# Six uses for a chunk's v product, spread over the steps, and an earlier start of the second phase

## The chip, the core and the metric

The kernel runs on one core of a Trainium2 chip. The core has five engines with a queue of instructions each: TensorE (PE; matmuls, with PEld for its weight loads), VectorE (DVE), ScalarE (ACT), GpSimd (POOL) and SyncE (SP), which here only issues DMAs. An engine takes its instructions in order and waits for others by semaphores. The metric is the device time of one execution in microseconds, the median of several.

## The reference

Inputs: q, k, v of 4 batches x 12 heads x 448 rows x 64; w_pre and w_post 12 x 12; w_in 768 x 2048, w_out 2048 x 768 and alpha 2048.

```
scores = q k^T / 8                                    per batch and head, 448 x 448
scores = einsum('bhij,hg->bgij', scores, w_pre)       heads mixed
attn   = softmax(scores over j)
attn   = einsum('bhij,hg->bgij', attn, w_post)        heads mixed again
x      = attn v, heads side by side                   1792 x 768
h      = x w_in
out    = (max(h, 0) + alpha min(h, 0)) w_out          1792 x 768
```

The weights w_in and w_out arrive as 64-bit floats and are rounded to 32 bits on the chip (the conversion).

## The kernel before

**First phase: attention.** A batch's 448 query rows are cut into four chunks (three of 120 rows, one of 97 of which the last 90 are used), 16 chunks in all, `ci`. A chunk is cut into groups of 10 rows x 12 heads, 180 in all, and a step `m` handles the two groups 2m and 2m+1. What a chunk and a step need is done by these functions:

- `qk(ci, p)`: score products of two heads of the chunk, a *use* of the bank pair `ps_s` (one buffer, two PSUM banks); `qk_out` lets ACT copy them to the SBUF tile `st`. Six per chunk.
- `relay`: a DMA that lays a group's scores out with (row, head) on the partitions, to `sr`, some steps ahead.
- `mix(m)`: the product with w_pre (TensorE) into one of two buffers of `ps_m`; `rmax` (DVE) and `exp` (ACT, two calls) follow; `norm` (DVE) folds the sum and w_post into a small factor `r`.
- `post(m)`, two steps later: the product of e and r, into `pa` (one buffer); `post_out` lets ACT copy it to the chunk's `at`.
- `pv(ci, half)`: the chunk's product with v, in two halves of three head pairs; both halves are uses of one `ps_s` tile, and `pv_out` copies both banks after the second half, each in one ACT copy of 3 x 120 columns. The result goes to the DRAM tensor `x2` by a DMA on SP.
- `convert`: the rounding of the weights on DVE, seven operations for each of 32 tiles, some two or three per step, fetched and stored (`wsc`) by SP.

`step(m)` records all this in a fixed order (the schedule is written by hand, `manual_schedule`); a step has two places for uses, one between mix and post and one after post. The table `places` says which use stands where: both halves of a chunk's `pv` in the step when its last group is through `post`, the six `qk` of the chunk ahead two to a step in the steps left. So there are three kinds of steps: with both halves of a `pv`, with two `qk`, and with nothing (L285 to L298).

**Second phase: the two layers.** It starts after the last step, in buffers that are opened once all pools of the first phase are closed. For each batch (`xs`, x transposed, 768 x 448) and each of 16 slices of 128 of the 2048 (a unit, 64 in all): `l1` multiplies with the slice of w_in, `act` applies the activation, `l2` multiplies with the slice of w_out and accumulates in six banks. Each value is split in a high and a low part, so each layer takes 18 matmuls per unit. `load_x` and `split_x` bring x from `x2` (DVE splits), `load_w` and `split_w` the weights from `wsc` (ACT writes the high part, POOL the low one). The loads of the first x stand on SP behind everything of the first phase.

Of the kernel before, what the change touches and what calls it, by code (L numbers as in the profile page):

```python
# [37 lines left out]
WARM = (12, 8)  # L38
X_FROM = 9
# [22 lines left out]
def talking_heads_prelu(ctx: ExitStack, tc: tile.TileContext, q, k, v, w_pre, w_post, mask, w_in, w_out, alpha, out):  # L62
# [18 lines left out]
    x2 = dpool.tile([NCC, 128, NT], F32, name="x2")  # L81
    wsc = dpool.tile([NFC, 128, 2 * DM], F32, name="wsc")
# [3 lines left out]
    p1 = ExitStack()  # L86
    pool = lambda name, bufs, **kw: p1.enter_context(tc.tile_pool(name=name, bufs=bufs, **kw))
    cvp = pool("cvp", 2)
    kp = pool("kp", 2)
    qp = pool("qp", 3)  # L90
    sp = pool("sp", 2)
# [8 lines left out]
    ps_m = pool("ps_m", 2, space=PSUM)  # L100
    ps_s = pool("ps_s", 1, space=PSUM)
    ps_a = pool("ps_a", 1, space=PSUM)
# [114 lines left out]
    def pv(ci, half):  # L217


        b, c = chunk_list[ci]  # L220
        cn = ROWS[c][1] * GI
        if half == 0:
            u_t["pv", ci] = ps_s.tile([128, 2, 512], F32, tag="s", name=f"x{ci}")
        ps = u_t["pv", ci]
        for cl in range(3):
            for s in range(NS):
                for t in range(2):
                    h = 2 * (3 * half + cl) + t
                    nc.tensor.matmul(ps[64 * t:64 * t + 64, half, cl * CW:cl * CW + cn], v_t[b][:, s, h * D:(h + 1) * D],  # L229
                                     a_t[ci][:, s, h, :cn], start=(s == 0), stop=(s == NS - 1))  # L230

    def pv_out(ci, half):

        if half == 0:
            return
        b, c = chunk_list[ci]
        r0, st = ROWS[c]
        c0, cn = CHUNKS[c][0] + r0, st * GI
        xe = xep.tile([128, NCC, CW], F32, tag="xe", name=f"xe{ci}")
        ps = u_t.pop(("pv", ci))  # L240
        for bank in range(2):
            src = ps[:, bank, :3 * CW].rearrange("p (c i) -> p c i", c=3)[:, :, :cn]
            nc.scalar.copy(xe[:, 3 * bank:3 * bank + 3, :cn].rearrange("p c (i g) -> p c i g", i=GI),
                           src.rearrange("p c (g i) -> p c i g", i=GI))
        later.append(lambda: nc.sync.dma_start(
            out=x2[:, :, b * S + c0:b * S + c0 + cn].rearrange("c p i -> p c i"), in_=xe[:, :, :cn]))
# [3 lines left out]
    def convert():  # L250
# [9 lines left out]
        def store_c(f, x, t):  # L260
            nc.sync.dma_start(out=wsc[f, :, x * DM:(x + 1) * DM], in_=t.bitcast(F32))
# [23 lines left out]
    places = {}  # L285
    for ci in range(NC):
        m = (first[ci + 1] - 1) // 2 + LAG + 1
        places[m, 0], places[m, 1] = ("pv", ci, 0), ("pv", ci, 1)
    for ci in range(1, NC):
        m1 = laid_out(first[ci]) - 1  # L290
        m0 = laid_out(first[ci - 1]) + 1 if ci > 1 else -1
        room = [(m, i) for m in range(m0, m1 + 1) for i in range(2) if (m, i) not in places]

        room.sort(key=lambda x: ((x[0], 1 - x[1]) in places or (x[0], 1 - x[1]) in room and x[1] == 1, x))
        room += [(m0 - 1, i) for i in range(2) if (m0 - 1, i) not in places]
        assert len(room) >= NP
        for p, x in enumerate(sorted(room[:NP])):
            places[x] = ("qk", ci, p)  # L298
# [10 lines left out]
    with tc.manual_schedule():  # L309
# [62 lines left out]
        def use(place, out):  # L372
            if place in places:
                f, *args = places[place]
                {"qk": (qk, qk_out), "pv": (pv, pv_out)}[f][out](*args)


        def step(m):
# [10 lines left out]
            use((m - 1, 1), 1)  # L389
            use((m, 0), 0)  # L390
# [13 lines left out]
            if live(m - LAG):  # L404
                post_out(m - LAG)
# [152 lines left out]
```

## Time and profile before

| | us |
|---|---|
| median of 3 runs | 931.94 (928.97 to 932.42) |
| profiled execution | 936.22, span 934.4 |
| first phase's steps, 35.7 to 418.8 | 383.1, TensorE busy 325.1 |
| from there to the second phase's steady run, 461.5 | 42.7 |
| second phase, 461.5 to 930.4 | 468.9, TensorE busy 468.9 |

A row of the timeline gives the start, the duration, the engine, the line, the operation with its output and inputs, how many instructions are merged in it, and in brackets the idle time before it with what ended it. "issue" as the releaser means that the engine waited for nothing that the profile shows. Matmuls of 32-bit floats in the first phase are recorded as two each, so a use of `qk` shows as 8 matmuls, one half of `pv` as 48, and `post` as 56. The spans of matmuls overlap; what one costs is better read from start to start.

### The profile page before, as it was taken

Reading aid. Unit: us, or ns where it says so; the run is one execution under the profiler, and the core shown is the slowest. Engines: PE = TensorE matmul, PEld = TensorE weight load, DVE = VectorE, ACT = ScalarE, POOL = GpSimd, SP = SyncE. Lnnn points to the kernel's source line nnn. Section 1 sums busy time; section 2 is a strip of 40 time slices with the busy share of each in tenths; the row PEclk is TensorE's granted clock in tenths of the full one; section 3 lists DMA queues with packets and bytes.
Section 4 is the critical chain, followed back from the end, with each engine's and each line's share of the span. In section 5 each row is a group of like instructions: output and inputs, shape, how many; then the busy total and the mean of one; then the engine's idle time right before and its main releaser. Section 6 shows DMA issues by size and latency. Waiting matters only on the chain.

```text
span 934.4 us, 23967 instructions
## 1 busy us (share of the span) xinstructions
PE 840.6 (90%) x10388; PEld 665.0 (71%) x10388; DVE 486.1 (52%) x856; ACT 438.1 (47%) x870; POOL 355.8 (38%) x315
## 2 busy tenths in 40 slices
PE   5779897798779989875699999999999999999998
PEld 3255563565555556545599999999999999999997
DVE  4758767587667878770522355223552236522222
ACT  1758877487757868753222233222233322322231
POOL 2323322132222323300554455555544455454442
PEclk9999999899999999999799999999999999999999
DMA  6999789988996897632770002000020000100001
GB/s 171 236 257 279 234 252 251 242 241 254 253 263 225 249 278 224 217 107 82 307 296 1 11 11 98 2 0 2 19 73 26 1 1 21 43 17 1 1 1 60
DMA packets 55158, 123.90 MB, mean 133 GB/s; under 512 B 26028, under 2 KB 32988, under 8 KB 55052
## 3 DMA queue, kind: packets, MB, share of 16 engines
q1 hardware_dynamic: 39846, 81.71, 29.2%
q0 software_dynamic: 14208, 37.56, 14.4%
q10 hardware_dynamic: 998, 3.09, 1.1%
q8 instruction: 82, 1.34, 0.6%
q14 instruction: 24, 0.20, 0.1%
HBM read 59.96 MB, written 23.62 MB: 89 GB/s over the span
## 4 chain that ended last, share of the span: by engine, by line
PE 69%; ACT 12%; issue 9%; DMA 5%; DVE 3%; POOL 1%; SPq 0%; ACTq 0%; POOLq 0%; DVEq 0%
PE acc L487 25%; PE h L462 25%; PE x L229 9%; ACT e L183 6%; PE s L146 4%; ACT st L154 4%; PE pa L205 3%; DMA sr<-st 3%; PE m L171 2%; ACT at L215 2%; DMA xr<-x 1%; POOL sr L163 1%; DMA wb<-in_w_post_dram 1%; DVE nm L176 1%; DVE ce L57 0%
## 5 line engine op out<-in xcount | busy, mean ns | idle before, releaser
L462 PE MATMUL h<-xs,wi 128*128 128x448 f32 x1152 | 251.1, 371 | 13.7 <-DVE xs L452 12.1
L487 PE MATMUL acc<-g,wo 128*128 128x448 f32 x1152 | 248.3, 368 | 0.0
L462 PEld LDWEIGHTS h<-xs,wi 128*128 128x128 f32 x1152 | 217.8, 189 | 36.7 <-issue 12.3
L487 PEld LDWEIGHTS acc<-g,wo 128*128 128x128 f32 x1152 | 216.3, 188 | 21.8
L163 POOL DMA_DIRECT2D sr<-st x174 | 108.2, 622 | 293.1 <-PE m L171 238.0
L440 POOL TENSOR_TENSOR wi<-wr,wi 128x768 fp32r<-128x768 f32 x64 | 118.6, 1853 | 263.4 <-ACT wi L439 263.4
L471 DVE TENSOR_SCALAR t<-h,alpha_sb 128x448 f32<-128x448 f32 x64 | 43.8, 684 | 245.4 <-PE h L462 245.4
L473 ACT CAST g<-t 128x448 fp32r<-128x448 f32 x64 | 36.3, 567 | 275.0 <-DVE t L472 275.0
L176 DVE TENSOR_REDUCE nm<-m 128x2 f32<-128x896 f32 x90 | 97.8, 1087 | 92.2 <-PE m L171 91.9
L205 PEld LDWEIGHTS pa<-r,e 64*64 64x64 f32 x5040 | 102.5, 138 | 55.4 <-issue 33.8
L440 POOL TENSOR_TENSOR wo<-wr,wo 128x768 fp32r<-128x768 f32 x64 | 123.9, 1935 | 7.6 <-ACT wo L439 5.9
L215 ACT COPY at<-pa 128x480 f32<-128x480 f32 x180 | 93.4, 576 | 59.1 <-PE pa L205 58.8
L205 PE MATMUL pa<-r,e 64*64 64x60 f32 x5040 | 106.8, 225 | 14.4 <-issue 9.0
L146 PE MATMUL s<-k,q 64*64 64x448 f32 (+2 forms) x768 | 100.7, 577 | 19.3 <-ACT st L154 11.9
L183 ACT ACTIVATE e<-m,nm 128x448 f32<-128x448 f32 x180 | 113.6, 644 | 5.1 <-DVE nm L176 3.0
L171 PE MATMUL m<-sr,wk 64*64 64x448 f32 x720 | 92.6, 566 | 18.5 <-ACT e L183 10.4
L229 PE MATMUL x<-at,v 128*64 128x120 f32 (+1 forms) x1536 | 86.7, 268 | 22.5 <-issue 19.8
L229 PEld LDWEIGHTS x<-at,v 128*64 128x64 f32 x1536 | 77.8, 140 | 36.6 <-issue 21.9
L154 ACT COPY st<-s 120x896 f32<-120x896 f32 (+1 forms) x93 | 84.8, 912 | 31.7 <-PE s L146 29.0
L439 ACT CAST wo<-wr 128x768 fp32r<-128x768 f32 x64 | 53.8, 841 | 62.3 <-PE acc L487 62.3
L146 PEld LDWEIGHTS s<-k,q 64*64 64x64 f32 (+2 forms) x768 | 22.6, 130 | 64.0 <-ACT st L154 42.6
L474 DVE TENSOR_TENSOR g<-t,g 128x448 fp32r<-128x448 f32 x64 | 40.7, 636 | 44.0 <-ACT g L473 44.0
(40 smaller groups left out, 484.8 us busy)
## 6 DMA issues: line engine op xcount, KB each, us to landing
sr<-st POOLq DMA_DIRECT2D x174, 210.0 KB, 7.0
cr<-in_w_in_dram SPq DMA_DIRECT2D x16, 768.0 KB, 6.6
cr<-in_w_out_dram SPq DMA_DIRECT2D x16, 768.0 KB, 7.8
wsc<-ct SPq DMA_DIRECT2D x32, 384.0 KB, 7.4
wr<-wsc SPq DMA_DIRECT2D x14, 768.0 KB, 10.2
xr<-x SPq DMA_DIRECT2D x24, 224.0 KB, 4.7
out_dram<-o SPq DMA_DIRECT2D x24, 224.0 KB, 2.0
k<-in_k_dram SPq DMA_DIRECT2D x21, 224.0 KB, 12.9
```

The source lines that it names most:

```text
L146: nc.tensor.matmul(ps[lo:hi, hf, :S], q_t[ci][r, p, lo:hi], k_t[b][r, p, :], start=True, stop=True)
L154: copy(dst[:cn, p], u_t.pop(("qk", ci, p))[:cn, :, :S])
L163: dma.dma_start(out=sr_t[n][SR0:SR0 + GP], in_=s_t[ci][r0:r0 + (GI - 1) * st + 1:st])
L171: nc.tensor.matmul(ps[hf:hf + 64, u, :S], wk[r, :], g[r, :], start=True, stop=True)
L176: nc.vector.tensor_reduce(out=nm, in_=m_t[m][:, :, :S], axis=AX.X, op=ALU.max, negate=True)
L183: nc.scalar.activation(out=e_t[m][:, u], in_=m_t[m][:, u, :S], func=AF.Exp, bias=nm_t[m][:, u:u + 1], scale=1.0, accum_out=se_t[m][:, u:u ...
L205: nc.tensor.matmul(dst[:, :, HI * u:HI * u + HI], e[h, u, 64 * jb:64 * jb + 64], r[h, u].rearrange("p (h i) -> p h i", h=H), start=True, s ...
L215: nc.scalar.copy(dst, pa[:, g, :NS * GP].rearrange("p (s i) -> p s i", i=GI))
L229: nc.tensor.matmul(ps[64 * t:64 * t + 64, half, cl * CW:cl * CW + cn], v_t[b][:, s, h * D:(h + 1) * D], a_t[ci][:, s, h, :cn], start=(s == ...
L440: nc.gpsimd.tensor_tensor(t[:, 1], w, t[:, 0], ALU.subtract)
L462: nc.tensor.matmul(ps[:, :S], w[:, tw, cc * 128:(cc + 1) * 128], x[:, tx, cc, :], start=(i == 0), stop=(i == 3 * NCC - 1))
L487: nc.tensor.matmul(accs[c][:, :S], w[:, tw, c * 128:(c + 1) * 128], g[:, tg], start=(f == 0 and i == 0), stop=(f == NFC - 1 and i == 2))
```

## The change

Two parts. First, `pv` of a chunk becomes six uses, one for each head pair, each with its own copy of one bank's 120 (or 90) columns into `xe`; the DMA to `x2` follows the sixth. A use may stand in any step of a window: for `pv` from the step after the chunk's last `post` to the step in which a tile of `at` is written again, for `qk` as before. An assignment (`cost`, six rounds over all uses) moves each use to the step of its window with the fewest others, preferring steps without its own kind. A step may now have any number of uses: the first between mix and post, the second after post, more behind the copy of the one before.

Second, the tensors `x2` and `wsc` become a tensor per batch and per slice. The pools that the scores and inputs used (`cvp`, `kp`, `qp`, `sp`) lie on the right side of SBUF and are closed at step M0 = 87; in their place open `xs0`, `xr`, `wi`, `wo`, `wr0`, `gp` of the second phase. The loads of the first batch's x and of three slices' weights stand there on SP, their splits in steps 88 and 89. After the last step, `post` 88, `l1` of unit 0, `post` 89, `l1` of unit 1 and the last chunk's six `pv` follow each other, then `l2` of unit 0 in another order of its banks.

```
-        for cl in range(3):
-            for s in range(NS):
-                for t in range(2):
-                    h = 2 * (3 * half + cl) + t
-                    nc.tensor.matmul(ps[64 * t:64 * t + 64, half, cl * CW:cl * CW + cn], ...)
+        ps = ps_s.tile([128, 2, 512], F32, tag="s", name=f"x{ci}_{i}")
+        for s in range(NS):
+            for t in range(2):
+                h = 2 * i + t
+                nc.tensor.matmul(ps[64 * t:64 * t + 64, 0, :cn], v_t[b][:, s, h * D:(h + 1) * D],
+                                 a_t[ci][:, s, h, :cn], start=(s == 0), stop=(s == NS - 1))
...
+        nc.scalar.copy(xe[:, i, :cn].rearrange("p (i g) -> p i g", i=GI),
+                       u_t.pop(("pv", ci, i))[:, 0, :cn].rearrange("p (g i) -> p i g", i=GI))
...
+        spread("qk", ci, laid_out(first[ci - 1]) + 1 if ci > 1 else -1, laid_out(first[ci]) - 1)
+        spread("pv", ci - 1, (first[ci] - 1) // 2 + LAG + 1, first[ci + 1] // 2 + LAG if ci + 1 < NC else NB - 1)
+    def cost(t, m):
+        there = [x[0] for x in tasks if x is not t and x[4] == m]
+        late = m == t[3] and t[0] == "pv" and len(there) > 1
+        return (late, 2 * len(there) + there.count(t[0]), m)
...
+            for u, v in zip(us[1:], us[2:]):
+                use(u, 1)
+                use(v, 0)
+            pending.extend(us[1:][-1:])
...
+        for m in range(-1, NB):
+            if m == M0:
+                ...
+                p1r.close()
+                open_early()
+                xq += [load_x(0, cc) for cc in range(3)]
+                load_w(0)
+                xq.append(load_x(0, 3))
+                load_w(1)
+                load_w(2)
+            step(m)
+            if m > M0:
+                for cc in range(3 * (m - M0 - 1), 3 * (m - M0)):
+                    split_x(0, cc, xq.pop(0))
+                    if cc + 4 < NCC:
+                        xq.append(load_x(0, cc + 4))
+                split_w(m - M0 - 1, 0)
+        p1m.close()
+        P2["h"] = pl("h", 2, space=PSUM, side="right")
+        while pending:
+            use(pending.pop(), 1)
+        norm(NB - 1)
+        post(NB - 2)
+        post_out(NB - 2)
+        split_w(0, 1)
+        ps = l1(0)
+        post(NB - 1)
+        post_out(NB - 1)
+        act(0, ps)
+        ps = l1(1)
+        for i in range(NP):
+            pv(NC - 1, i)
+            pv_out(NC - 1, i)
+        act(1, ps)
+        for f in later:
+            f()
+        ...
+        load_w(3)
+        load_w(4)
+        split_w(1, 1)
+        split_w(2, 0)
+        l2(0)
```

TensorE's queue before, in the middle of the first phase: two steps without a use, then a step with both halves of a chunk's v product and the mix of the next (m is mix, pa is post, x the v product, s the score product; x24 are 24 matmuls of the program).

```order
L171 MATMUL m_5307<-sr_116,wk 64x448 x2
L171 MATMUL m_5307<-sr_117,wk 64x448 x2
L205 MATMUL pa<-r_5259,e_5195 64x12x5 x28
L171 MATMUL m_5359<-sr_110,wk 64x448 x2
L171 MATMUL m_5359<-sr_111,wk 64x448 x2
L205 MATMUL pa<-r_5316,e_5263 64x12x5 x28
L171 MATMUL m_5414<-sr_112,wk 64x448 x2
L171 MATMUL m_5414<-sr_113,wk 64x448 x2
L229 MATMUL x_5420<-at_4997,v_119 64x120 x24
L205 MATMUL pa<-r_5367,e_5320 64x12x5 x28
L229 MATMUL x_5420<-at_4997,v_119 64x120 x24
```

The same engine after, in the same part: two steps, each with one score product ahead of post and a sixth of a v product behind it.

```order
L173 MATMUL m_5257<-sr_130,wk 64x448 x2
L173 MATMUL m_5257<-sr_131,wk 64x448 x2
L148 MATMUL s_3_5264<-k_3692,q_4833 64x448 x2
L148 MATMUL s_3_5264<-k_3692,q_4833 56x448 x2
L207 MATMUL pa<-r_5201,e_5136 64x12x5 x28
L230 MATMUL x_1_5311<-at_4828,v_136 64x90 x8
L173 MATMUL m_5329<-sr_132,wk 64x448 x2
L173 MATMUL m_5329<-sr_133,wk 64x448 x2
L148 MATMUL s_4_5336<-k_3692,q_4833 64x448 x2
L148 MATMUL s_4_5336<-k_3692,q_4833 56x448 x2
L207 MATMUL pa<-r_5272,e_5205 64x12x5 x28
L230 MATMUL x_2_5383<-at_4828,v_136 64x90 x8
```

The v product has left its own step and stands where a step had a second score product or nothing.

SP's queue before, at the seam of the phases: the stores of the last three chunks' x and of the last converted weights, then the second phase's loads of x (xr) and weights (wr).

```order
L245 DMA x_57<-xe_5925 128x6x120
L261 DMA wsc<-ct_0_5815 128x768
L245 DMA x_57<-xe_6267 128x6x120
L245 DMA x_57<-xe_6424 128x6x90
L261 DMA wsc<-ct_1_5973 128x768
L447 DMA xr_0_6473<-x_57 128x448
L447 DMA xr_1_6475<-x_57 128x448
L447 DMA xr_2_6477<-x_57 128x448
L447 DMA xr_3_6479<-x_57 128x448
```

The same queue after.

```order
L245 DMA x_3_60<-xe_5676 128x6x120
L261 DMA wsc_76<-ct_0_5948 128x768
L261 DMA wsc_76<-ct_1_6077 128x768
L461 DMA xr_0_6282<-x_0_57 128x448
L461 DMA xr_1_6284<-x_0_57 128x448
L461 DMA xr_2_6286<-x_0_57 128x448
L446 DMA wr_6288<-wsc_61 128x1536
L461 DMA xr_3_6290<-x_0_57 128x448
L446 DMA wr_6292<-wsc_62 128x1536
L446 DMA wr_6294<-wsc_63 128x1536
L245 DMA x_3_60<-xe_5981 128x6x120
```

Four loads of x and three of weights have moved ahead of the stores of the last three chunks.

TensorE's queue after, at the seam (h is the first layer's product, 18 matmuls a unit): the last uses of the chunk before the last, then posts and first-layer products in turn, and the last chunk's uses.

```order
L230 MATMUL x_4_6454<-at_5943,v_137 64x120 x8
L207 MATMUL pa<-r_6371,e_6317 64x12x5 x28
L230 MATMUL x_5_6501<-at_5943,v_137 64x120 x8
L207 MATMUL pa<-r_6466,e_6375 64x12x5 x28
L476 MATMUL h_6564<-xs_6281,wi_6450 128x448 x18
L207 MATMUL pa<-r_6529,e_6468 64x12x5 x28
L476 MATMUL h_6619<-xs_6281,wi_6518 128x448 x18
L230 MATMUL x_0_6638<-at_6351,v_137 64x90 x8
L230 MATMUL x_1_6649<-at_6351,v_137 64x90 x8
```

Before, all h stood behind the last chunk's x; now two units' h stand between the posts and ahead of that x.

## Rows read from the trace of the kernel before

**Rows 1.** Windows by stage: stretch, length, each engine's busy us, clock, DMA share, GB/s.
```profile
35.70:418.80 383.10, 325.09 (x7524) 208.15 (x7516) 282.32 (x562) 275.67 (x628) 104.42 (x168) 0.97 0.86 240
418.80:437.70 18.90, 14.58 (x424) 12.92 (x424) 2.93 (x11) 8.18 (x21) 0.00 (x0) 1.00 0.08 23
...
461.50:930.40 468.90, 468.90 (x2269) 425.63 (x2268) 173.06 (x236) 138.35 (x199) 236.01 (x125) 1.00 0.10 37
```

**Rows 2.** Timeline of TensorE, three kinds of steps: start, duration, line, operation, wait.
```profile
299.71 2.68 PE L229 MATMUL x<-at,v 128*64 128x120 f32 x48
302.32 0.98 PE L171 MATMUL m<-sr,wk 64*64 64x448 f32 x8
...
306.19 0.93 PE L171 MATMUL m<-sr,wk 64*64 64x448 f32 x8
307.39 0.98 PE L146 MATMUL s<-k,q 64*64 64x448 f32 x8 [0.28 <-ACT st L154]
308.20 1.09 PE L205 MATMUL pa<-r,e 64*64 64x60 f32 x56
...
310.23 0.93 PE L171 MATMUL m<-sr,wk 64*64 64x448 f32 x8
...
314.28 0.93 PE L171 MATMUL m<-sr,wk 64*64 64x448 f32 x8
...
316.73 0.98 PE L171 MATMUL m<-sr,wk 64*64 64x448 f32 x8 [0.60 <-ACT e L183]
```

**Rows 3.** Waits of TensorE: total us, times, longest.
```profile
PE x L229 <- issue: 19.8, 9, 4.5
...
PE s L146 <- ACT st L154: 11.9, 33, 1.1
...
PE pa L205 <- issue: 9.0, 7, 2.2
PE m L171 <- DMA sr<-st: 7.1, 4, 5.1
```

**Rows 4.** Timeline of TensorE, two neighbouring issue waits.
```profile
270.25 0.63 PE L229 MATMUL x<-at,v 128*64 128x120 f32 x7 [1.69 <-issue]
...
278.56 1.86 PE L205 MATMUL pa<-r,e 64*64 64x60 f32 x55 [2.11 <-issue]
```

**Rows 5.** DMA queues of the page: packets, MB, share of 16 engines.
```profile
q8 instruction: 82, 1.34, 0.6%
```

**Rows 6.** Groups of the page: busy us, mean ns, idle before.
```profile
L440 POOL TENSOR_TENSOR wi<-wr,wi 128x768 fp32r<-128x768 f32 x64 | 118.6, 1853 | 263.4 <-ACT wi L439 263.4
...
L154 ACT COPY st<-s 120x896 f32<-120x896 f32 (+1 forms) x93 | 84.8, 912 | 31.7 <-PE s L146 29.0
L439 ACT CAST wo<-wr 128x768 fp32r<-128x768 f32 x64 | 53.8, 841 | 62.3 <-PE acc L487 62.3
```

**Rows 7.** Tile xe: ns min/median/max, first and last start, forms.
```profile
L243 ACT COPY xe<-x x32: 384/459/466, 69.7 to 438.0; 128x360 f32<-128x360 f32 x24, 128x270 f32<-128x270 f32 x8
```

**Rows 8.** Timeline of TensorE at the seam.
```profile
418.81 0.98 PE L171 MATMUL m<-sr,wk 64*64 64x448 f32 x8 [1.20 <-ACT e L183]
...
433.71 3.94 PE L229 MATMUL x<-at,v 128*64 128x90 f32 x96 [1.13 <-ACT at L215]
449.78 0.71 PE L462 MATMUL h<-xs,wi 128*128 128x448 f32 x1 [12.12 <-DVE xs L452]
```

**Rows 9.** The chain that ended last, its last long piece.
```profile
922.96 7.45 PE acc L487 x36
```

**Rows 10.** Timeline of SP's queue at the seam.
```profile
426.98 11.79 SPq L245 DMA_DIRECT2D x<-xe  x2
...
439.40 13.68 SPq L447 DMA_DIRECT2D xr<-x  x6
```

**Rows 11.** Tile xs: ns min/median/max of cast and subtraction.
```profile
L452 DVE CAST xs<-xr x24: 379/386/1787, 447.8 to 806.5; 128x448 fp32r<-128x448 f32 x24
L453 DVE TENSOR_TENSOR xs<-xr,xs x24: 624/2153/2162, 449.7 to 807.0; 128x448 fp32r<-128x448 f32 x24
```

More of the change, by code (lines that the diff above doesn't have):

```diff
@@ L38 @@
 WARM = (12, 8)
+W_EARLY = 3
 X_FROM = 9
@@ L238, in pv_out @@
         c0, cn = CHUNKS[c][0] + r0, st * GI
[L239 to L246, printed above, removed]
+        if i == 0:
+            xe_t[ci] = xep.tile([128, NCC, CW], F32, tag="xe", name=f"xe{ci}")
+        xe = xe_t[ci]
+        nc.scalar.copy(xe[:, i, :cn].rearrange("p (i g) -> p i g", i=GI),
+                       u_t.pop(("pv", ci, i))[:, 0, :cn].rearrange("p (g i) -> p i g", i=GI))
+        if i == NCC - 1:
+            later.append(lambda: nc.sync.dma_start(
+                out=x2[b][:, :, c0:c0 + cn].rearrange("c p i -> p c i"), in_=xe[:, :, :cn]))
     later = []
@@ L281, in laid_out, with spread @@
         return max(n // 2 - RAHEAD - 1, 0 if n < first[1] else 3)
[L285 to L288, printed above, removed]
+    uses, tasks = {}, []
+    def spread(f, ci, m0, m1):
+        tasks.extend([f, ci, m0, m1, m0 + i % (m1 - m0 + 1)] for i in range(NP))
     for ci in range(1, NC):
[L290 to L298, printed above, removed]
+        spread("qk", ci, laid_out(first[ci - 1]) + 1 if ci > 1 else -1, laid_out(first[ci]) - 1)
[4 more added lines that the diff above has]
+        return (late, 2 * len(there) + there.count(t[0]), m)
+    for _ in range(NP):
+        for t in tasks:
+            t[4] = min(range(t[2], t[3] + 1), key=lambda m: cost(t, m))
+    number = {}
+    for f, ci, _, _, m in sorted(tasks, key=lambda t: t[4]):
+        i = number[f, ci] = number.get((f, ci), -1) + 1
+        uses.setdefault(m, []).append((f, ci, i))
+    for x in uses.values():
+        x.sort(key=lambda u: (u[0] == "pv", u))
     for ci, (b, c) in enumerate(chunk_list):
@@ L388, in step @@
                 f()
-            use((m - 1, 1), 1)
-            use((m, 0), 0)
+            while pending:
+                use(pending.pop(), 1)
+            us = uses.get(m, [])
+            for u in us[:1]:
+                use(u, 0)
             if live(m - 1):
@@ L409, in step @@
                 done += 1
-        last = max(m for m, _ in places)
-        for m in range(-1, max(NB + LAG, last + 1) + 1):
-            step(m)
-        for _ in conv:
-            pass
-        for f in later:
-            f()
-        p0.close()
-        p1.close()
         p2 = ctx.enter_context(ExitStack())
@@ L492, in l2 @@
                     nc.sync.dma_start(out=out[c * 128:(c + 1) * 128, b * S:(b + 1) * S], in_=o)
-        NU = B * NFC
-        xq = [load_x(0, cc) for cc in range(4)]
-        load_w(0, nc.scalar)
-        load_w(1, nc.scalar)
-        for cc in range(NCC):
-            split_x(0, cc, xq.pop(0))
-            if cc == 1:
-                split_w(0, 0)
-            if cc + 4 < NCC:
-                xq.append(load_x(0, cc + 4))
-        load_w(2)
-        for u in range(NU + 1):
+        M0 = NB - 3
+        assert all(m < M0 or u[0] == "pv" for m, us in uses.items() for u in us)
+        xq = []
+        for m in range(-1, NB):
+            if m == M0:
+                assert done == conv_steps and relayed == NG
+                for _ in conv:
+                    pass
+                now, later[:] = list(later), []
+                for f in now:
+                    f()
[15 more added lines that the diff above has]
+        P2["h"] = pl("h", 2, space=PSUM, side="right")
+        while pending:
+            use(pending.pop(), 1)
+        norm(NB - 1)
[12 more added lines that the diff above has]
+        for f in later:
+            f()
+        p0.close()
+        p1.close()
+        open_late()
+        load_w(3)
[3 more added lines that the diff above has]
+        l2(0)
+        NU = B * NFC
+        for u in range(2, NU + 1):
             b, f = divmod(u, NFC)
```

67 lines of the change are left out of this document (33 added, 34 removed).

## The prediction

> **What bounds the kernel now.** I read the windows by stage first, then TensorE's timeline inside the first phase, then its waits, then the timeline around the seam between the phases. By stage [rows 1], the second phase (461.5 to 930.4 us) has TensorE busy for the whole 468.9 us: a unit of 36 matmuls costs 7.44 us, the last being the chain's last piece [rows 9], and nothing around it matters. Nothing of the change touches that loop. What can move is the first phase (35.7 to 418.8: 86 steps in 383.1 us, TensorE 325.1 busy, DVE 282.3, ACT 275.7, DMA share 0.86) and the seam (418.8 to about 460).
>
> In the first phase three kinds of step alternate [rows 2]. The pieces on TensorE: mix 0.92 (306.19 to 307.39 less a wait of 0.28), score product 0.81 (307.39 to 308.20), post 1.1, half a v product 2.61 (299.71 to 302.32), so a sixth 0.87. A step with both halves of a chunk's v product is 7.2 us by its pieces, one with two score products lasts 4.04 (306.19 to 310.23), one without a use 2.45 (314.28 to 316.73). All three kinds are nearly TensorE's own time; the two-score step also loses 0.28 us to ACT's copy of the scores (0.91 us long [rows 6]). So evening the steps out removes little work from TensorE.
>
> What is not TensorE's own are its waits put down to "issue": 19.8 us in 9 waits before v products and 9.0 us in 7 before post [rows 3], 28.8 us. They are regular. Between the ones at 270.25 and 278.56 [rows 4] stand 127 recorded matmuls, with their weight loads 254 instructions. The queue of kind "instruction" moved 1.34 MB in 82 packets [rows 5], 16 KB each; I read the waits as TensorE arriving at the end of a block of its program before the next has landed, in a phase whose DMA engines are nearly full. The 8.3 us between those two waits is then how long a block took. About 16 of the phase's 59 block ends show a wait.
>
> **Part 1, the spread uses.** The product of a chunk goes from two uses with 48 recorded matmuls to six with 16; the matmuls are the same. Copies go from 2 to 6 per chunk. Two of 360 columns take 0.46 us each and two of 270 take 0.38 [rows 7]: 0.08 us for 90 columns, so 120 columns cost about 0.25 and a chunk pays 1.5 instead of 0.92, some 9 us on ACT over the phase. ACT has 107 us free there [rows 1], so I cost it at nothing on the path; if ACT were the bound it would cost the 9.
>
> Counting the assignment's steps among the same 86: 41 with one score and one v product, 13 with two scores, 14 with two v products, 7 with two scores and one v, 1 with one score and two v, 6 with one v, 3 with one score, 1 without. With the pieces above: a mixed step is 0.92 + 0.81 + 1.1 + 0.87 = 3.7, taken as 3.75; two scores 4.04 as measured; two v 3.8; a third use waits until ACT has copied the second one behind post's two copies, about 1.1 us more, so 4.04 + 0.87 + 1.1 = 6.0, taken as 5.9; one and two v 5.3; a lone v 3.3 (DVE's conversions set it), a lone score 3.1, none 2.45. The sum is 41 x 3.75 + 13 x 4.04 + 14 x 3.8 + 7 x 5.9 + 5.3 + 6 x 3.3 + 3 x 3.1 + 2.45 = 338 us. To it I add 3.5 us of the first steps' waits for relayed scores (7.1 us in all [rows 3], they stay) and 4 us for waits of post's copy into a new chunk's buffer, which now stands behind the last v product of the chunk two before: 345.5. Before, without issue waits, it was 383.1 - 28.8 = 354.3. **Term A: -9 us**; between 0 (every saved wait comes back as another) and -16 (no added wait shows).
>
> A mixed step leaves DVE 282.3/86 = 3.3 us of work in 3.75 and ACT 3.3, so both have cover, but little: a conversion that waits long for its DMA would now be felt.
>
> **Term B, the block waits.** The blocks are as many as before. TensorE now uses them evenly, one in about 5.8 us; before it burned 128 recorded instructions in an empty step of 2.45 us (two steps a block, 4.9 us) and used one in about 7 in a two-score step. The relays, two a step, were bunched in the same empty steps. Both even out, which shortens the excess of a block's landing over its use. Against that, the same bytes go through in less time: the DMA share of 0.86 over 383 us is 330 us of full engines, over 357 us it is 0.92. Bounds: all 28.8 us go, or 5 more come. Two-score steps, the nearest to the new steps in pace, show a wait seldom (278.56 is one [rows 4]), so I take off somewhat under half: **-12 us**.
>
> [...]
>
> **Part 2, the seam.** Before, mix 89 starts at 418.81 and TensorE ends at 922.96 + 7.45 = 930.41 [rows 8, 9], 511.6 us later, of which 64 units x 7.44 = 476.2 are the second phase. So 35.4 us go for the rest of the first phase and the gap: TensorE ends its last v product at 437.65 and starts the second phase at 449.78, because SP holds the x loads behind the two last stores of x: the stores issue from 426.98 over 11.79 us, the loads start at 439.40, and the wait at 449.78 ends with the first cast of x [rows 8, 10].
>
> After, the loads of x and of three weights stand ahead of the stores of the last three chunks on SP; ahead of them are the store of chunk 12 and the last two stores of converted weights, done some two steps before mix 89. The 3.2 MB land while DMA is nearly idle (share 0.08 after 418.8 [rows 1]). DVE gets 12 and ACT and POOL 3 operations each in the last steps. POOL's take 1.85 us each [rows 6], but the first unit comes behind post 88 on TensorE, about 11 us after mix 89, and the last x cast is done by then (six pairs at 0.39 + 0.62 us are 6 us of DVE; the subtraction takes up to 2.16 beside POOL [rows 11], and with three of the six that slow it is 10.7).
>
> TensorE from mix 89 to the first l2: mix 0.92, chunk 14's product 5.24, four posts 4.4, chunk 15's product 3.94 (its row, 96 matmuls, 433.71 [rows 8]), two l1 units 7.44: 21.9 us. One bank pair for the uses makes eight products wait for the copy before them: 0.25 us and two handovers, about 0.45 each, 3.6 in all (bounds by rows 3: 11.9/33 = 0.36 and the longest, 1.1, so 2.9 to 8.8). ACT's weight cast (0.84 [rows 6]) stands before one of those copies, and post 88 waits for copies: 1.1. After l2 of the first unit, l1 of the third wants POOL's low part of its weights, which stands behind another POOL operation and behind ACT's last x copies: about 1.5 us. The end is then 418.81 + 26.6 + 476.2 - 7.44 + 1.5 = 915.7 where it was 930.4. **Term C: -15 us**, between -9 (handovers at 1.1) and -18.
>
> **Sum.** -9 - 12 - 15 = -36. Against the profiled execution of 936.2 us (span 934.4 and 1.8 around it) that is 900; the median of the runs shown is 931.94, 4.3 lower, so 896. What can be told from no change here is 0.5%, 4.7 us.
>
> **The rivals.**
> 1. Forecast, as summed: 896 (885 to 904). Chance 0.57.
> 2. The block waits stay whole, since DMA is nearly full at any pace; B is 0: 896 + 12 = 908 (904 to 921). For it: share 0.86 before, more after. Against it: the bunched steps are gone. [...] Chance 0.20.
> 3. The block waits vanish: 896 - 17 = 879 (870 to 885). For it: an even pace for TensorE and for the DMA demand. Against it: waits seen in evenly paced steps. Chance 0.13.
> 4. Slower: handovers. The uses share one pair of banks, and there are 64 more of them in 90 steps. If each costs TensorE the longest wait seen, 1.1 us [rows 3], that is 70 us against 36 gained: 966. It decides from 33 uses on (36/1.1). For it: two-score steps already wait 0.28. Against it: in a mixed step post (1.1 us) or mix stands between a use and the next, longer than a 0.25 us copy, and ACT is 72% busy. Chance 0.05.
> 5. No change: the loads do not arrive in the last steps (a late conversion store holds SP), and A and B come to nothing: 927 to 937. Chance 0.05.
>
> The range reaches from case 3's low end to case 2's high end, 872 to 921. Faster 0.90, same 0.05, slower 0.05.
>
> **What would show it.** Right: TensorE's timeline in the first phase shows steps of 3.7 to 4.0 us without a v step over 7; issue waits on TensorE fall from 28.8 to about 17; the gap of 12.1 us at the seam is gone and the first h matmul comes about 11 us after the last mix, beside posts. The second phase keeps 3.72 us for 18 matmuls. Wrong: mixed steps over 4.3 us with waits for xe copies (case 4), issue waits at 28 or more (case 2), or TensorE waiting for x casts or for weights at the seam (case 5).

## The result: 920.7 us, and the profile after

| | before | after |
|---|---|---|
| median us (four runs each, same chip) | 932.18 (928.97 to 939.86) | 920.72 (916.65 to 924.58) |
| ratio, 95% interval | | 0.9889 (0.9843 to 0.9935) |
| first mix of step 2 to mix 89, profiled execution | 35.73 to 418.81: 383.1 | 38.35 to 419.14: 380.8 |
| mix 89 to TensorE's end | 511.6 | 497.9 |

The kernel is faster by about 11 us, a third of the 36 forecast. By stage, after (stretch, length, busy us of TensorE, its weight loads, DVE, ACT, POOL; clock, DMA share, GB/s), beside [rows 1]:

```profile
38.35:419.14 380.79, 327.45 (x7529) 208.34 (x7529) 285.39 (x566) 288.37 (x685) 106.87 (x168) 0.97 0.89 242
...
460.00:917.00 457.00, 456.98 (x2227) 417.61 (x2225) 169.44 (x232) 135.74 (x195) 229.61 (x122) 1.00 0.10 37
```

The second phase still keeps TensorE busy throughout. The first phase is only 2.3 us shorter, and mix 89 starts within 0.4 us of where it did, with the DMA share up from 0.86 to 0.89. TensorE's waits after (total us, times, longest), beside [rows 3]:

```profile
PE pa L207 <- issue: 22.0, 17, 3.3
PE m L173 <- DMA sr<-st: 7.8, 2, 4.1
PE x L230 <- ACT st L156: 7.5, 8, 1.0
PE s L148 <- ACT st L156: 6.4, 16, 1.0
PE x L230 <- issue: 3.7, 4, 1.3
PE m L173 <- issue: 3.2, 2, 2.6
...
PE x L230 <- ACT xe L242: 3.2, 9, 0.4
...
PE s L148 <- issue: 1.2, 1, 1.2
```

The four rows put down to issue are 30.1 us where [rows 3] had 28.8; most of it now stands before post, which has 56 of the 88 matmul records of a mixed step. Waits for ACT's copies of scores or of the product (the rows with st and xe) come to 17.1 us in 33 waits; the same kinds before, of which [rows 3] shows 11.9, come to 13.7 in 37. What went down is the wait of the mix for the exponential, which the rows ahead of the prediction leave out; before and after:

```profile
PE m L171 <- ACT e L183: 10.4, 16, 1.2
```
```profile
PE m L173 <- ACT e L185: 1.5, 3, 1.0
```

Within the first phase all waits for ACT together fell from 21.2 to 14.5 us. A mixed step (one score product, one sixth of a v product) in TensorE's timeline after, read from start to start:

```profile
389.57 0.98 PE L173 MATMUL m<-sr,wk 64*64 64x448 f32 x8
390.38 0.93 PE L148 MATMUL s<-k,q 64*64 64x448 f32 x8
391.13 1.10 PE L207 MATMUL pa<-r,e 64*64 64x60 f32 x56
392.33 1.04 PE L230 MATMUL x<-at,v 128*64 128x120 f32 x16
393.30 0.98 PE L173 MATMUL m<-sr,wk 64*64 64x448 f32 x8
```

It lasts 3.73 us, the forecast's 3.75. So the steps are what the change says; the time did not follow them. Around the seam, after, beside [rows 8]:

```profile
419.14 0.98 PE L173 MATMUL m<-sr,wk 64*64 64x448 f32 x8 [1.02 <-ACT e L185]
...
430.63 2.70 PE L476 MATMUL h<-xs,wi 128*128 128x448 f32 x12
...
434.71 0.47 PE L476 MATMUL h<-xs,wi 128*128 128x448 f32 x1 [1.37 <-DVE xs L466]
...
444.64 0.84 PE L230 MATMUL x<-at,v 128*64 128x90 f32 x16 [0.38 <-ACT xe L242]
...
450.12 3.92 PE L502 MATMUL acc<-g,wo 128*128 128x448 f32 x18
...
455.42 3.51 PE L476 MATMUL h<-xs,wi 128*128 128x448 f32 x16 [0.99 <-POOL wi L454]
```

The first product of the second phase starts 11.5 us after mix 89, with the first parts of x already there; the wait of 12.12 us [rows 8] is gone, and 1.37 and 0.99 us stand in its place. The chain ends, after, with its last piece as before [rows 9], now ending at 916.99:

```profile
909.54 7.45 PE acc L502 x36
```

### The profile page after: what moved, and what is told of

Its sections match the earlier page's. It is cut to its first block, busy times and chain, and to the rows that moved or that the text cites. A ratio compares the mean times of both kernels' runs of the same rounds, so it can differ in the third digit from the quotient of the medians.

```text
span 920.8 us, 24000 instructions
## 1 busy us (share of the span) xinstructions
PE 846.3 (92%) x10388; PEld 665.9 (72%) x10388; DVE 487.1 (53%) x856; ACT 450.6 (49%) x934; POOL 357.4 (39%) x315
## 3 DMA queue, kind: packets, MB, share of 16 engines
q0 software_dynamic: 14208, 37.56, 15.5%
## 4 chain that ended last, share of the span: by engine, by line
PE 65%; issue 17%; POOL 5%; ACT 5%; DMA 4%; DVE 3%; POOLq 0%; DVEq 0%; ACTq 0%; SPq 0%
PE acc L502 25%; PE h L476 25%; PE x L230 5%; POOL sr L165 4%; PE s L148 4%; PE m L173 4%; ACT st L156 4%; DMA sr<-st 3%; PE pa L207 2%; DMA x<-xe 1%; ACT e L185 1%; DVE nm L178 1%; DMA wb<-in_w_post_dram 1%; POOL wo L454 0%; DVE ce L58 0%
## 5 line engine op out<-in xcount | busy, mean ns | idle before, releaser
L476 PE MATMUL h<-xs,wi 128*128 128x448 f32 x1152 | 248.0, 368 | 2.6 <-DVE xs L466 1.4
L165 POOL DMA_DIRECT2D sr<-st x174 | 110.6, 636 | 290.9 <-PE m L173 219.9
L230 PE MATMUL x<-at,v 128*64 128x120 f32 (+1 forms) x1536 | 99.5, 272 | 18.7 <-ACT st L156 7.5
L173 PE MATMUL m<-sr,wk 64*64 64x448 f32 x720 | 95.4, 586 | 12.4 <-DMA sr<-st 7.8
L148 PEld LDWEIGHTS s<-k,q 64*64 64x64 f32 (+2 forms) x768 | 27.0, 134 | 61.8 <-ACT st L156 23.9
## 6 DMA issues: line engine op xcount, KB each, us to landing
k<-in_k_dram SPq DMA_DIRECT2D x21, 224.0 KB, 10.4
```

The lines of the kernel that those rows point to most:

```text
L148: nc.tensor.matmul(ps[lo:hi, hf, :S], q_t[ci][r, p, lo:hi], k_t[b][r, p, :], start=True, stop=True)
L165: dma.dma_start(out=sr_t[n][SR0:SR0 + GP], in_=s_t[ci][r0:r0 + (GI - 1) * st + 1:st])
L173: nc.tensor.matmul(ps[hf:hf + 64, u, :S], wk[r, :], g[r, :], start=True, stop=True)
L230: nc.tensor.matmul(ps[64 * t:64 * t + 64, 0, :cn], v_t[b][:, s, h * D:(h + 1) * D], a_t[ci][:, s, h, :cn], start=(s == 0), stop=(s == NS - 1))
L476: nc.tensor.matmul(ps[:, :S], w[:, tw, cc * 128:(cc + 1) * 128], x[:, tx, cc, :], start=(i == 0), stop=(i == 3 * NCC - 1))
```

## The experiments

Times are medians of six runs or more, ratios (with their 95% intervals) against the kernel before on the same chip, unless said otherwise. Labels such as e3 stand for the run's full label. "Phase" means the first phase, from the start of step 2's mix to mix 89.

**Each part alone.** In e1_spread the kernel before gets part 1 (six uses and the assignment) and keeps its seam. In e2_seam the kernel after keeps part 2 and gets back `pv` in two halves at the old places.

> Part 1 alone: six uses per chunk, spread by the assignment, second phase and its seam as before. Theory D (in the first phase the DMA engines are nearly full, so that TensorE's saved time comes back as waits for blocks of its program and for relays): about 930, within 5 us of before, TensorE's issue waits near 30 us. Rival G (the spread gains its 20 us and the early loads of the second phase give them back): about 912. Rival S (the added handovers cost what the even steps save; then steps of one score and one v product are over 4.2 us where nothing is waited for).

> Part 2 alone: v products in two halves at their old places, the second phase's first loads, weights and buffers two units early. Theory D: the whole gain of the changed kernel, 12 to 16 us, about 918. Rival G: more than that, since the spread would be the one that loses: below 912.

e1 took 932.3 us, ratio 1.0013 (0.9973 to 1.0052); e2 921.2, ratio 0.9881 (0.9829 to 0.9933). The phase lasted 384.9 and 385.2 us. Both came out nearly as theory D has it: the seam is the whole gain (10.8 us of 11.5); the spread is worth nothing that can be measured. Waits of TensorE in e1:

```profile
PE pa L205 <- issue: 28.1, 15, 4.7
...
PE x L228 <- issue: 4.5, 3, 1.9
```

With some smaller ones these are 34.3 us, more than before the spread.

**Less DMA, in either order.** Only the first two raw weight tiles of 768 KB are fetched and used again for all others, so 30 fetches are left out:

```
+                if i < 2:
+                    raw_2.append(cvp.tile([128, DM], I64, tag=f"cr{i}", bufs=1, ...))
+                    nc.sync.dma_start(out=raw_2[i], in_=(w_in, w_out)[x][f])
+                raw_c[i] = raw_2[i % 2]
```

> The changed kernel with the weights' raw data fetched for the first two tiles only, so that the 30 later fetches of 768 KB are left out (23 of some 96 MB of the first phase) while DVE still converts 32 tiles from the two that stand there; the output is not the reference's. Theory D: issue waits on TensorE fall under 10 us and the first phase from 381 us for 86 steps to about 335, so 870 to 880. Rival F (a block of the program takes its 5 to 10 us whatever else the DMA engines do): issue waits stay near 30 and the time near 915.

> The kernel before with the same 30 fetches left out; the output is not the reference's. Theory D: the issue waits go here too, 383 us for 86 steps become about 350, so 895 to 900, and the changed kernel with the same cut is then 20 to 30 us faster than this one (seam 14, spread 10 or more). Rival F: near 930.

e3 (after, cut) took 887.8 us, ratio 0.9507 (0.9459 to 0.9556); e4 (before, cut) 898.8, ratio 0.9623 (0.9575 to 0.9670). Window of the phase and issue waits of e3:

```profile
38.80:387.55 348.75, 317.25 (x7528) 203.38 (x7528) 284.54 (x566) 288.58 (x685) 106.28 (x168) 0.99 0.70 197
```
```profile
PE pa L207 <- issue: 7.5, 6, 2.5
...
PE m L173 <- issue: 3.1, 1, 3.1
```

and of e4:

```profile
36.18:387.95 351.77, 312.27 (x7524) 198.42 (x7517) 282.06 (x562) 275.65 (x628) 105.30 (x168) 1.00 0.71 194
```
```profile
PE x L229 <- issue: 7.8, 5, 3.1
...
PE pa L205 <- issue: 2.9, 3, 1.1
```

With the share at 0.70 the issue waits fall to 10.6 us (e4: 10.7), the same in both orders, although e4 has the bunched uses. So the bunching of the uses did not cause the waits. e3 and e4 differ by 11.0 us, about what the seam alone is worth; the 20 to 30 us that theory D expected between them did not come, nor its 870 to 880 for e3. The spread gains little here too: the phases differ by 3.0 us.

**Finer fetches, fewer stores, smaller relays.** e5_fine fetches each raw tile by four DMAs of 32 partitions, one ahead of each of the first four operations on the tile before. e8_nostore leaves out 30 of the 32 stores of rounded weights (the second phase then reads slice 0 for all). e14_halfrelay relays 5 of 10 rows from the ninth group on.

```
e5    +  for p in range(0, 128, 32)[part]:
      +      nc.sync.dma_start(out=raw_c[i][p:p + 32], in_=(w_in, w_out)[x][f, p:p + 32])
e8    +  if f == 0:
             nc.sync.dma_start(out=wsc[f][:, x * DM:(x + 1) * DM], in_=t.bitcast(F32))
e14   +  k = GI if n < NSR else GI // 2
```

> The changed kernel with each raw weight tile fetched by four DMAs of 192 KB, one ahead of each of the first four conversion operations of the tile before, in place of one of 768 KB: same bytes, a quarter of the burst. Theory V (the sum of the traffic delays the blocks of TensorE's program): no change, 916 to 925, issue waits on TensorE near 30 us. Rival Q (a single long DMA ahead of a block delays it): issue waits halve, about 905.

> The changed kernel without 30 of the 32 stores of converted weights (all slices of the second phase read the first slice's, so the output is not the reference's): 11.8 MB of writes leave the first phase, half the bytes of the 30 fetches. Theory V by bytes: half of 33 us, about 904. If only reads from HBM matter: near 920.

> The changed kernel with relays of 5 rows in place of 10 from the ninth group on (the other half of each relay's tile keeps old scores, so the output is not the reference's): about 18 MB from SBUF to SBUF leave the POOL queue of the first phase, some 68 us of engine time by the queue's share (15.5% of 920.8 us for 37.56 MB); SP's queue and the reads from HBM stay. Theory E (block waits follow the engines' busy time, whatever the traffic): 0.37 us for 1 us, so 20 to 28 us off, 893 to 901. Rival H (it is the reads of the raw weights from HBM, or SP's queue held up by them, that delay the blocks): 915 or more.

e5: 943.2 us, ratio 1.0165 (1.0136 to 1.0194). e8: 917.9, 0.9872 (0.9829 to 0.9915). e14: 896.6, 0.9656 (0.9612 to 0.9701). The phase of e5, and its largest issue waits:

```profile
37.86:437.28 399.42, 329.73 (x7527) 210.75 (x7529) 284.95 (x567) 288.48 (x684) 105.34 (x168) 0.96 0.95 231
```
```profile
PE pa L207 <- issue: 38.5, 17, 4.6
...
PE x L230 <- issue: 4.9, 2, 2.5
```

The same bytes in smaller pieces kept the DMA engines busier (0.95) and made the issue waits 48.1 us; neither expectation had a slower kernel. The phase of e14 and its issue wait:

```profile
34.86:389.14 354.28, 315.50 (x7528) 202.00 (x7529) 284.81 (x566) 288.38 (x685) 106.90 (x168) 1.00 0.76 210
```
```profile
PE pa L208 <- issue: 10.1, 7, 4.3
```

Here every fetch from HBM stays and only transfers between SBUF tiles were halved, and the waits shrink as in e3 (12.0 us with a smaller row), as theory E has it and rival H does not. e8 by its median can't be told from after, as its second expectation has it (only reads from HBM matter); e14, where no such read is gone, speaks against that reason. Now these kernels together. *Engine time* is the phase's length times its DMA share (after: 380.79 x 0.89 = 339). *Excess* is the phase's length less the sum, over its steps, of each step's shortest time in three profiled kernels of the same order: 347.6 us for the old places (before, e2, e4), 342.7 for the spread (after, e1, e3).

| | e3 | e4 | e14 | e8 | before | e1 | e2 | after | e5 |
|---|---|---|---|---|---|---|---|---|---|
| engine time | 244 | 250 | 269 | 319 | 329 | 331 | 335 | 339 | 379 |
| excess | 6 | 4 | 12 | 28 | 35 | 42 | 38 | 38 | 57 |
| issue waits | 10.6 | 10.7 | 12.0 | 24.9 | 28.8 | 34.3 | 32.0 | 30.1 | 48.1 |

From e3 to e5 the excess grows by 51 us over 135 us, 0.38 per us of engine time, for fetches and relays alike and in whichever order the uses stand. Three limits: e3 and e4 are among the kernels that give the shortest times, so their excess is small by construction; the medians of the runs, which need no such sum, give 32.9 us for 95 (after less e3), 24.1 for 70 (after less e14) and 22.5 for 40 (e5 less after), 0.34 to 0.56 per us. For stores it is not shown, since the profiled execution of e8 took 907.8 us, 10 less than its median. And small differences do not order the kernels: e6, e7, e9, e16 and e17, below, have 315 to 339 us of engine time, an excess of 30 to 44 and issue waits of 24.5 to 34.7.

**The clock behind the waits.** The excess is not waits alone. From after to e3 the phase loses 32 us, of which 19.5 are issue waits; but TensorE is also busy 10.2 us less with the same matmuls (327.45 and 317.25), and from before to e4 12.8 less (325.09 and 312.27). A wait of after, with the rows behind it and their window:

```profile
143.64 1.77 PE L173 MATMUL m<-sr,wk 64*64 64x448 f32 x8 [2.59 <-issue]
```
```profile
143.20:146.60 3.40, 2.96 (x21) 1.59 (x23) 1.10 (x2) 0.00 (x0) 0.88 (x2) 0.50 1.06 257
```

The mix takes 1.77 us where it took 0.98 above: the granted clock of that window is 0.50. Such stretches add up to 24 us of the phase before and after, 31 in e5, 7 in e3, 3 in e4 and e14, and none in e10 and e11, which have no issue waits. In before and after each of them stands behind an issue wait, but one, behind a wait of 3.71 us for a relay. So an issue wait can cost more than its own length: 7 of the 16 in before and 5 of the 24 in after have such a stretch behind them, of 3.4 us each.

**Where the waits stand.** e7_shift adds 16 warming matmuls at the program's start (`WARM = (12, 24)` for `(12, 8)`), 32 recorded instructions with their loads; one profile and one time.

> The changed kernel with 16 more warm-up matmuls before the first mix (32 instructions with their loads, done while TensorE waits for the first relays, up to 2 us more). If the issue waits are block ends of TensorE's program, every one of them moves 32 recorded instructions ahead in the steps, and the distances between them stay multiples of some 253 recorded instructions. If they come from something at a fixed place of the steps, they stay where they were. Time 915 to 928.

It took 923.7 us. Issue waits in the timeline of after:

```profile
67.89 1.69 PE L207 MATMUL pa<-r,e 64*64 64x60 f32 x54 [1.20 <-issue]
...
76.83 0.40 PE L207 MATMUL pa<-r,e 64*64 64x60 f32 x12 [3.01 <-issue]
...
91.72 0.47 PE L207 MATMUL pa<-r,e 64*64 64x60 f32 x16 [2.94 <-issue]
```

and of e7:

```profile
64.00 1.76 PE L230 MATMUL x<-at,v 128*64 128x120 f32 x14 [2.59 <-issue]
...
73.10 0.73 PE L207 MATMUL pa<-r,e 64*64 64x60 f32 x30 [1.43 <-issue]
...
87.97 0.79 PE L207 MATMUL pa<-r,e 64*64 64x60 f32 x32 [1.58 <-issue]
```

Counted in the kernel's own matmuls and weight loads (without the added warming ones), seven waits that both have stand in after at 1196, 1450, 1704, 1960, 3736, 3992, 5008, in e7 at 1164, 1418, 1672, 1928, 3704, 3960, 4976: each 32 earlier, with steps of 254 or 256 between the first four. Counted with the semaphore instructions of TensorE's queue too, all 249 issue waits in the profiles of this case stand at places 192 to 194 modulo 256. The waits belong to places in TensorE's program, the ends of blocks, not to any work.

The traces also hold the packets of the queue of kind "instruction" (81 of 16 KB in after, for 20,776 recorded matmuls and weight loads), and with them the time when each block landed. The window of after's longest wait, 272.75 to 276.03, has one such packet:

```profile
q8 instruction: 1, 0.02, 2.5%
```

It started at 273.22 and ended at 274.54. All 249 waits end 1.3 to 1.8 us after the end of such a packet. For the blocks that are used in the phase (59, in e10 43), in us, the median and in brackets the values that a tenth of them lie below and above:

| | before | after | e5 | e14 | e4 | e3 | e10 |
|---|---|---|---|---|---|---|---|
| TensorE's use of a block, without the wait at its end | 6.0 (4.8, 6.9) | 5.8 (4.4, 7.3) | 6.0 (4.6, 8.3) | 5.6 (4.4, 7.4) | 5.8 (4.7, 6.9) | 5.7 (4.3, 7.0) | 9.5 (8.7, 10.9) |
| from a block's start to the end of the next one's packet | 4.0 (1.9, 6.3) | 3.9 (1.7, 6.3) | 3.8 (2.1, 7.2) | 2.5 (1.3, 5.5) | 2.5 (1.1, 5.0) | 2.2 (1.1, 4.6) | 1.8 (0.3, 5.1) |

The packet itself took 1.1 to 1.3 us (median) in each of them; what changes is how late it starts. The spread made the use of the blocks no more even and let them land hardly sooner. With less DMA (e14, e4, e3) they land sooner; in e5 the median stays and the latest tenth comes later.

**A slower TensorE.** e10_post128 computes post by 16 matmuls with up to 128 columns of weights instead of 28 with 64; e11 is the kernel before with the same post. e13_qk128 does the same for the score products, 2 matmuls of up to 120 columns instead of 4 of 64.

```
e10, e11  -  for jb in range(NJ):  ... e[h, u, 64 * jb:64 * jb + 64]
          +  for s in range(NS):   ... e[h, u, 128 * s:128 * s + n]
e13       -  for lo in range(0, cn, 64):
          +  for lo, hi in ((0, cn),):
```

> The changed kernel with post in 16 matmuls of 128 columns of weights (the last of each four with 64) in place of 28 of 64: 32 recorded matmuls for 56, so 128 instructions for 176 in a step of one score and one v product, 43 blocks of the program for 59. Theory E: TensorE uses a block in 7.5 us in place of 5.6 and mostly finds the next one there, issue waits fall from 30 to under 12 us, time 890 to 902. [...] If block ends had nothing to do with it: 920.

> The kernel before with the same post. Theory E: its waits fall as well, in the steps without a use above all: 905 to 915; the spread uses are then worth their 5 us and the seam 14, so about 15 to 20 us above the changed kernel with this post. [...]

> The changed kernel with a score product in 2 matmuls of up to 120 columns of weights in place of 4 of up to 64 (4 recorded for 8). [...] Theory E: a product takes 0.4 to 0.75 us, TensorE has 5 to 35 us less to do, and a third or more of it comes back as waits for blocks and relays, which are as many per byte as before: 900 to 917. [...]

e10: 961.6 us, 1.0345 (1.0297 to 1.0393). e11: 968.7, 1.0420 (1.0366 to 1.0473). e13: 921.8, 0.9929 (0.9903 to 0.9955). One post in e10, start to start 2.14 us where it was 1.1, the queue that brings instructions (packets, MB, share), 81 packets in after, and the window of e10's phase:

```profile
300.28 2.21 PE L207 MATMUL pa<-r,e 64*128 64x60 f32 x32
302.42 1.04 PE L230 MATMUL x<-at,v 128*64 128x120 f32 x16
```
```profile
q8 instruction: 64, 1.05, 0.5%
```
```profile
36.48:457.68 421.20, 405.81 (x5462) 268.22 (x5463) 286.80 (x569) 284.86 (x684) 107.43 (x168) 1.00 0.78 221
```

e10 shows no issue wait at all, e11 none either, although the share, 0.78, is above that of e14 (0.76), which has 12.0 us of them. But post takes twice as long, and the times that theory E expected of both did not come. The longer posts give TensorE 86 x 1.04 = 89 us more work in the phase; the phase is 40 us longer. Of the rest 30 are the issue waits, and some 11 by an estimate (half of the 22 us that TensorE worked in after's stretches at a clock of 0.50) the lower clock; e10 has neither. In e10 every block of the phase landed 4.5 us or more before TensorE came to it (e11: 1.7). In e13 (a score product 0.95 us from start to start, where it was 0.81):

```profile
305.57 1.02 PE L147 MATMUL s<-k,q 64*120 64x448 f32 x4
306.52 1.15 PE L206 MATMUL pa<-r,e 64*64 64x60 f32 x56
```

The product is slower, not faster as theory E has it, whose 0.4 to 0.75 us no run shows: TensorE is busy 16.7 us longer in the phase (344.1), and the kernel takes 1 us more than after, less than either interval can tell; its issue waits are 26.0 us. So in this phase neither work taken off TensorE nor such work added moves the end one for one.

**x stored in longer runs.** e9_x2c lays x out by chunks in DRAM, so that a full chunk's store has runs of 2880 bytes and not 480, and a load takes two DMAs; e12 and e15 combine it with e10 and e13.

> The changed kernel with x kept in DRAM per chunk, so that a store of x writes one run of 2880 bytes a partition in place of six of 480, and the second phase's loads gather from four chunks (two DMAs a load). Bytes stay, the first phase's packets under 512 bytes go to the second. Theory E (block waits follow the time that the DMA engines are busy, not the bytes: about 0.37 us of waits for 1 us of it, by the runs so far): if the 12,288 short runs cost some 30 us of engine time, 8 to 11 us come off, about 911. If short runs cost no engine time worth naming: 920.

> Both edits on the changed kernel. Theory E: little left to wait for, the first phase's 86 steps near 343 to 350 us, 885 to 895; the x layout adds less here than alone, since the waits are mostly gone.

> The same with x kept in DRAM per chunk (one run of 2880 bytes a partition for six of 480, loads gather in the second phase). The layout alone gave 917.9 with runs from 912.8 to 932.8, no clear gain. Theory E: 0 to 8 us below the kernel with the score product's edit alone.

917.9 us, 0.9866 (0.9812 to 0.9921); 963.2, 1.0351 (1.0301 to 1.0400); 921.8, 0.9907 (0.9873 to 0.9942). Engine time in e9 was 331 us. None of the three can be told from its partner without the layout; theory E had expected about 911 and 885 to 895 of the first two.

**Rounding moved to the second phase**, whose DMA share is 0.10 and whose DVE is idle for more than half. The last slices' raw weights are fetched and rounded there and are never stored; three slices with five DVE operations per unit (e6_late3), or two slices with three (e16_late2, and e17_late2_x2c with e9's layout).

```
+LATE = 2
-        todo = [(f, x) for f in range(NFC) for x in range(2)]
+        todo = [(f, x) for f in range(NFC - LATE) for x in range(2)]
...
+                for _ in range(3):          # after act of a unit
+                    next(late, None)
```

> The changed kernel with the last three of the 16 weight slices converted in the second phase, straight into the SBUF tiles that are read there (five DVE operations a unit from the third unit on, output buffers cut from 5 to 3): 6 fetches of 768 KB and 6 stores of 384 KB leave the first phase, 7.1 MB of some 96. Theory V: 33 us were gained for 23.6 MB, so about 10 us here, 911, as long as the second phase keeps 7.44 us a unit. Rival Q: 920, bursts being what they were. If DVE is late for TensorE in the units 2 to 10, the gain is lost there.

> The changed kernel with the last two weight slices converted in the second phase, three DVE operations a unit (with three slices and five operations the first phase gave 4 us and the second lost 12, TensorE waiting for ACT's g behind DVE). 4.7 MB leave the first phase, some 12 us of engine time, so 4 to 5 us by 0.38 us each. Theory E: 914 to 918 if the second phase keeps 7.44 us a unit; 920 or more if DVE is still late there.

> The same with x kept in DRAM per chunk. Alone the layout gave 3 us, within the scatter. Theory E: 911 to 917, the fastest version with the reference's output so far.

e6: 922.5 us, 0.9890 (0.9848 to 0.9933), where 911 was expected. Its profiled execution took 927.9, so its stages are a rough guide: mix 89 came 6.5 us sooner, at 412.67, but from there to TensorE's end it took 508.7 us (497.9 after). ACT's half of the activation waited up to 7.9 us for DVE there (4.5 after), and TensorE 7.1 us in six waits for ACT, as in these:

```profile
490.54 4.17 PE L523 MATMUL acc<-g,wo 128*128 128x448 f32 x18 [1.33 <-ACT g L508]
...
518.63 5.54 PE L523 MATMUL acc<-g,wo 128*128 128x448 f32 x18 [2.12 <-ACT g L508]
```

e16: 915.9 us, 0.9795 (0.9742 to 0.9848), mix 89 at 412.69. Both, this and e17, are where theory E expected them. e17: 913.5 us, 0.9771 (0.9719 to 0.9823), the fastest version here; its interval lies below that of after, but e16 and e17 can't be told apart. In e17 the issue waits are still there:

```profile
PE pa L208 <- issue: 24.0, 11, 4.4
...
PE x L231 <- issue: 6.5, 3, 4.0
```

## Why the prediction failed

The end of TensorE moved by 930.41 - 916.99 = 13.4 us in the profiled executions. By the forecast's steps:

| | forecast | measured |
|---|---|---|
| A, the steps' own time | -9 | -4.9 (347.6 to 342.7) |
| B, the block waits | -12 | +2.6 (excess 35.5 to 38.1; issue waits 28.8 to 30.1) |
| C, the seam | -15 | -13.75 (511.6 to 497.85) |
| the phase's start | 0 | +2.6 (35.73 to 38.35) |
| sum | -36 | -13.4 |

- **What bounds the kernel** was read rightly for the second phase and wrongly for the first. "All three kinds are nearly TensorE's own time", said of the steps, leaves out 0.60 us in the row beside it (316.73, for ACT's exponential), one of 16 such waits, 10.4 us in all. What makes the phase longer than its steps' shortest times are the block waits and the lower clock behind them, and these follow how busy the DMA engines are.
- **Term B is the step that failed.** The prediction put it so: "Both even out, which shortens the excess of a block's landing over its use." The blocks' places were read rightly (e7), and that a wait is for a block that has not landed (the packets). But neither side evened out: the middle eight tenths of the blocks were used in 4.8 to 6.9 us before and in 4.4 to 7.3 after, and the next one landed at a median of 4.0 and 3.9 us. And the waits don't come from bunched uses: e3 and e4 have 10.6 and 10.7 us with the uses spread or bunched. They follow the engine time, which no part of the change lowers (329 us before, 339 after). The sentence against it stood beside it, the same bytes in less time; the runs bear this one out. Term B should have been 0 or a little more, as rival 2 had it; its range, 904 to 921, holds the result at its upper edge. That the whole range, 872 to 921, holds it too is luck: its end was rival 2's.
- **Term A** was right in sign and too large. Kinds of step after, by the medians of those without an issue wait: mixed 3.73 (forecast 3.75), two scores 3.56 (4.04), two v 3.93 (3.8), two scores and a v 5.74 (5.9). These were near; the error is on the side of before, where I took all that isn't issue wait for the steps' own time (354.3) and the shortest times sum to 347.6; in 354.3 is also what the lower clock costs, for which the forecast had no term. And what A saved, mostly waits for ACT (21.2 to 14.5 us), came back as other waits: e1 has A, 5.5 us more of issue waits, and is no faster.
- **Term C** was right in size (-13.75 for -15), and with it the reading that the second phase's loads at SP's end made the gap. The first h product came 11.5 us after mix 89 (about 11), POOL's low part cost 0.99 us (1.5), a handover 0.33 to 0.38 (0.45). Not foreseen were the 1.37 us for a cast of x.
- **Rival 4**, the handovers, is refuted: waits of the product for `xe` are 3.2 us in 9, the longest 0.4.
- **Two readings** were off without changing a term: the forecast's own phase is 383.1 - 9 - 12 = 362 us, not 357, so 330 us of engine time are a share of 0.91; and a two-score step has 160 recorded instructions, so a block of such steps takes 6.5 us, not about 7.

Shown: the waits stand at fixed places of TensorE's program (e7), end when a block has landed (the packets), vanish when a block takes longer to use (e10, a median of 9.5 us where after has 5.8; e11), and grow with the DMA engines' busy time, by fetches or relays (e3, e4, e5, e14). Only argued: that a block's packet starts late because it queues behind the data; no record tells what an engine did before it took the packet. Open is the 2.6 us by which step 2 starts later; kernels with the spread start it between 33.65 and 38.8, the others between 35.7 and 37.3, so it may be scatter.

## What to carry to other kernels

Before costing a rearrangement of an engine's work, ask what its "issue" waits follow: if they stand at even distances in the program (here multiples of 256 instructions) while the DMA engines are nearly full (here 0.86 to 0.95), expect the engine's saved time to come back as such waits; here less DMA time took two thirds of them away (30.1 to 10.6 us in e3), and a slower use of the program all of them, at a higher price (e10, 41 us slower). Price a change of such a stage by the engine time that it removes (here about 0.4 us per us, for changes of 40 us and more), and move transfers to a stage that leaves the engines idle, in an amount that the other engines there can take. A gap that one queue's order makes (here SP's loads behind its stores) was worth its whole length (a wait of 12.12 us, a gain of 13.75), and could be forecast to a us or two.

## What the runs showed of the hardware

- All 249 issue waits of TensorE stand at places 192 to 194 modulo 256 of its queue, and TensorE went on 1.3 to 1.8 us after a 16 KB packet of the instruction queue had ended, which took 1.1 to 1.3 us (median). I read this as a program that came in blocks of 256 instructions.
- Behind 7 of the 16 such waits in before and 5 of the 24 in after the granted clock was 0.50 for a stretch; such stretches make 24 us of the phase in each. With 3 and 7 us of it TensorE was busy 13 and 10 us less with the same matmuls (e4 and e3).
- The 28 matmuls of after's post (56 recorded, 64 columns of weights and 60 moving columns) took 1.1 us, 20 ns a record. The 16 of e10's, with up to 128 columns of weights (32 recorded), took 2.14 us, 67 ns a record. The score product, with 448 moving columns, took 0.81 us by 4 matmuls of up to 64 columns of weights and 0.95 by 2 of up to 120 (e13).
- A 768 KB fetch cut into four of 32 partitions, issued one after another over four operations, moved the same bytes with more engine time, 379 us against 339 over the phase, and cost 22 us of the whole. Not all of it is the fetches' own: the unchanged relays' packets (q0) took 16.9% of 937.3 us where they took 15.5% of 920.8.
- Stores in runs of 480 or of 2880 bytes made no difference that can be told (920.7 and 917.9 us).
